# Token sums of the softmax over tokens for batches 0 and 1: added on GpSimd instead of by eight matmuls

## The chip, the cores and the metric

One core of one Trainium2 chip. The metric is the device time of the kernel in microseconds (us). Small differences are read twice: as ratios of timed runs with a 95% interval, and as moments inside the traces. Engine names in the profile: PE is TensorE, PEld its weight loads, DVE VectorE, ACT ScalarE, POOL GpSimd, SP SyncE (SPq its queue of transfer issues).

## The reference

`x` is 8 batches x 8 heads x 512 tokens x 64, `state` 8 x 8 x 32 x 64. What matters is the second attention, from state to tokens (two lines of the reference are joined here):

```python
scores2 = scale * np.matmul(state, x.transpose(0, 1, 3, 2))
a2 = np.exp(scores2 - scores2.max(-1, keepdims=True))
a2 /= a2.sum(-1, keepdims=True) + 1e-09      # sum over the 512 tokens
sread = np.matmul(a2, x)
```

The result (with the first attention's) goes through a gated layer `(sigmoid(x @ w_gate) * (x @ w_val)) @ w_out`, which is nearly all of the matmul work.

## The kernel before

Tokens lie as 128 partitions x 4 tokens, so the sum over 512 tokens is a sum over 4 in the partition and over 128 partitions. TensorE does the latter with a matrix of ones. `E1s` are the exponentials in fp32, `Ebs` the same in bf16.

```python
def at_Eb(b):                                  # GpSimd casts E1 to bf16
    Ebs[b] = ap_.tile((128, 4, 2, 4, Ns), BF, name="Eb")
    for c in range(4):
        nc.gpsimd.tensor_copy(Ebs[b][:, c], E1s[b][:, c])
...
def sr_mm(b, place):
    ...
    if b in Es:                                # batches 2 to 7: summed over c before
        terms = [(e, Es[b][:, k, e]) for e in range(2) for k in range(2)]
    else:                                      # batches 0 and 1
        terms = [(e, Eb[:, c, e]) for e in range(2) for c in range(4)]
    for i, (e, rhs) in enumerate(terms):
        nc.tensor.matmul(sm, ones[:, e], rhs, start=(i == 0), stop=(i == len(terms) - 1))
    for j in range(4):                         # then the unnormalised read, 16 matmuls
        ...
```

Each engine runs its instructions in program order. The order around the place, with cuts marked `...` (the comments are mine, here and above):

```python
    gv_glu(0, 4)
    at_Eb(0)
    load_x(2, nc.gpsimd)
    load_wo(0)
    load_wo(1)
    load_wo(2)
    load_x(3, nc.gpsimd)
    gv_glu(0, 5)
    ...
    sw_visit(1, 512, 512, 0)
    ...
    sr_mm(1, AT)                # TensorE's sum for batch 1
    ...
    gv_mm(1, 1, GV)             # GLU pair of feature block 1
    ...
    sr_mm(0, OU)                # and for batch 0, some 9 us later
    ...
    pad(2, 6)                   # GpSimd: two copies
    cast_x(2, pool, 0, 4)       # GpSimd: x of batch 2 to bf16
    cast_x(2, pool, 4, 4)
    cast_x(3, pool, 0, 4)
    cast_x(3, pool, 4, 4)
    at_xT_dma(2)                # SyncE: four transposing transfers, then the scores of batch 2
    at_xT_dma(3)
```

The softmax here doesn't subtract the row's maximum and nothing guards it: scores larger than these inputs give would overflow.

Of the kernel before, what the change touches and what calls it, by code (L numbers as in the profile page):

```python
# [8 lines left out]
FP = mybir.dt.float32  # L9
BF = mybir.dt.bfloat16  # L10
AF = mybir.ActivationFunctionType
ALU = mybir.AluOpType
# [4 lines left out]
def kernel(  # L17
# [14 lines left out]
    nc = tc.nc  # L32
    B, H, S, D = x.shape
    Ns = state.shape[2]
# [11 lines left out]
    ap_ = ctx.enter_context(tc.tile_pool(name="ap", bufs=2))  # L46
# [19 lines left out]
    Es, E1s, Ebs, abs_, aTs, SWs, glus = {}, {}, {}, {}, {}, {}, {}  # L66
    vec, act, pool = nc.vector.tensor_copy, nc.scalar.copy, nc.gpsimd.tensor_copy


    def load_x(b, eng, parts=1, hold=None):  # L70
        xf = stg.tile((128, H, 4, D), FP, name="xf")
        if hold is not None:

            hold.memset(xf[:, 0, 0, 0:1], 0.0)
        v = x[b].rearrange("h (p c) d -> p h c d", c=4)
        n = H // parts
        for i in range(parts):
            eng.dma_start(xf[:, n * i:n * i + n], v[:, n * i:n * i + n])
        xfs[b] = xf
# [16 lines left out]
    def load_wo(q):  # L96
        nc.gpsimd.dma_start(wo[:, 4 * q:4 * q + 4],
                            moe_w_out.rearrange("(k p) n -> p k n", p=128)[:, 4 * q:4 * q + 4])
# [57 lines left out]
    def n_tok(b, e):  # L156

        if e == 0:
            held["E4", b] = ap_.tile((128, 2, 4, Ns), FP, name="E4")
        nc.vector.tensor_reduce(held["E4", b][:, e].rearrange("p j n -> p (j n)"),  # L160
                                E1s[b][:, :, e].rearrange("p c j n -> p (j n) c"), AX.X, ALU.add)

    def n_split(b, k):

        if k == 0:
            Es[b] = ap_.tile((128, 2, 2, 4, Ns), BF, name="Es")
            nc.vector.tensor_copy(Es[b][:, 0], held["E4", b])
        else:
            nc.vector.tensor_tensor(Es[b][:, 1], held["E4", b], Es[b][:, 0], ALU.subtract)
# [105 lines left out]
    def sw_cp(b, lo, w, e, cp):  # L275
        cp(*sw_left.pop((b, lo, w, e)))  # L276


    def n_of(b):
        return 512 if b < B else B * Ns  # L280
# [21 lines left out]
    def gv_glu(b, f):  # L302
        if b not in glus:
            glus[b] = fp.tile((128, NF, n_of(b)), BF, name="glu", bufs=2, padded_shape=(128, NF, 512))
        nc.vector.scalar_tensor_tensor(glus[b][:, f], held["th", b, f], 1.0, held["gv", b, f][1], ALU.add, ALU.mult)  # L305
# [192 lines left out]
    load_wo(1)  # L498
    load_wo(2)
    load_x(3, nc.gpsimd)  # L500
    gv_glu(0, 5)
    sw_cp(1, 512, 1, 1, vec)
    sw_visit(1, 512, 512, 0)
# [72 lines left out]
    for b in range(1, B + 1):  # L576
        nb = b + 1 if b + 1 < B else None
        for f in range(NF):
# [14 lines left out]
            if nb is not None:  # L593
# [15 lines left out]
                if f in (6, 7):  # L609
                    n_tok(nb, f - 6)  # L610
                    if f == 7:
                        n_split(nb, 0)
                elif f == 8:
                    n_split(nb, 1)
                elif f == 9:
                    sr_mm(nb, AT)
                    sr_inv(nb)
                    if b == 1:
                        sr_fin(nb)
                elif f == 10 and b > 1:  # L620
                    sr_fin(nb)
# [48 lines left out]
```

## Time and profile before

| | before |
|---|---|
| time, median of 3 runs | 229.8 us (228.96 to 230.15) |
| TensorE busy | 95% of the span of 227.5 us |
| GpSimd busy | 20% |
| ones-matmuls of batches 0 and 1 | 2 x 8, holding TensorE's stream for 0.46 and 0.45 us |
| last transpose of batch 2 landed | 46.88 us, in one profile |

TensorE's busy share is close to full, so read the moments, not the shares: when does each block of TensorE's stream start, and what did it wait for. The lines are in the prediction.

### The profile page before, as it was taken

Reading aid. Unit: us, or ns where it says so; the run is one execution under the profiler, and the core shown is the slowest. Engines: PE = TensorE matmul, PEld = TensorE weight load, DVE = VectorE, ACT = ScalarE, POOL = GpSimd, SP = SyncE. Lnnn points to the kernel's source line nnn. Section 1 sums busy time; section 2 is a strip of 40 time slices with the busy share of each in tenths; the row PEclk is TensorE's granted clock in tenths of the full one; section 3 lists DMA queues with packets and bytes.
Section 4 is the critical chain, followed back from the end, with each engine's and each line's share of the span. In section 5 each row is a group of like instructions: output and inputs, shape, how many; then the busy total and the mean of one; then the engine's idle time right before and its main releaser. Section 6 shows DMA issues by size and latency. Waiting matters only on the chain.

```text
span 227.5 us, 4735 instructions
## 1 busy us (share of the span) xinstructions
PE 215.7 (95%) x1831; PEld 111.6 (49%) x1856; DVE 141.4 (62%) x234; ACT 131.0 (58%) x246; POOL 44.4 (20%) x78
## 2 busy tenths in 40 slices
PE   7568999999999999999999999999999999999994
PEld 7453345444454545444544454454445444466743
DVE  2599889967448855886488638874687433422301
ACT  3677877647476566746675666656755444423311
POOL 1499930060033001500060006000200000000001
PEclk9999999999999999999999999999999999999999
DMA  6999999943699252725282431243122111111113
GB/s 213 354 176 191 233 264 242 152 80 69 145 287 248 41 132 101 231 46 124 87 252 43 83 116 46 81 83 116 46 72 69 48 46 49 67 73 46 49 35 104
DMA packets 37990, 28.09 MB, mean 123 GB/s; under 512 B 20976, under 2 KB 33136, under 8 KB 37968
## 3 DMA queue, kind: packets, MB, share of 16 engines
q1 hardware_dynamic: 32464, 21.31, 35.3%
q0 software_dynamic: 5360, 6.42, 14.8%
q8 instruction: 14, 0.23, 0.4%
q14 instruction: 8, 0.07, 0.2%
q10 hardware_dynamic: 144, 0.07, 0.1%
HBM read 18.35 MB, written 8.91 MB: 120 GB/s over the span
## 4 chain that ended last, share of the span: by engine, by line
PE 76%; DMA 11%; POOL 5%; SPq 3%; issue 2%; ACT 1%; DVE 0%; POOLq 0%; ACTq 0%
PE outp L321 35%; PE gvp L290 28%; DMA xf<-in_x_dram 8%; PE gvp L293 5%; PE swp L238 4%; DMA xT<-xb 3%; SPq L128 2%; PE srp L215 1%; POOL Eb L145 1%; PE Sp L134 1%; PE outp L341 1%; POOL wg L83 1%; POOL ab L175 1%; POOL xb L103 1%; POOL wv L94 1%
## 5 line engine op out<-in xcount | busy, mean ns | idle before, releaser
L305 DVE SCALAR_TENSOR_TENSOR glu<-th,gvp 128x512 bf16<-128x512 f32 (+1 forms) x108 | 70.2, 657 | 63.9 <-ACT th L300 48.2
L300 ACT ACTIVATE th<-gvp 128x512 f32<-128x512 f32 (+1 forms) x108 | 61.6, 575 | 62.5 <-PE gvp L290 51.2
L290 PE MATMUL gvp<-aT,SW 128*128 128x512 bf16 x384 | 96.3, 379 | 0.2
L321 PE MATMUL outp<-wo,glu 128*128 128x512 bf16 x371 | 95.1, 379 | 1.3 <-issue 0.2
L290 PEld LDWEIGHTS <-SW 128*128 128x128 bf16 x384 | 36.2, 98 | 45.1 <-issue 4.2
L321 PEld LDWEIGHTS <-glu 128*128 128x128 bf16 x396 | 37.4, 98 | 40.7 <-issue 0.4
L276 ACT CAST SW<-swp 128x512 bf16<-128x512 f32 (+1 forms) x78 | 42.2, 582 | 4.2 <-PE swp L238 2.9
L145 POOL CAST Eb<-E 128x256 bf16<-128x256 f32 x32 | 12.4, 429 | 96.2 <-ACT E L139 96.2
L325 ACT ACTIVATE res<-outp 128x512 f32<-128x512 f32 x33 | 19.7, 598 | 17.1 <-PE outp L321 17.1
L103 POOL CAST xb<-xf 128x1024 bf16<-128x1024 f32 (+1 forms) x13 | 14.6, 1147 | 20.8 <-DMA xf<-in_x_dram 20.8
L276 DVE CAST SW<-swp 128x512 bf16<-128x512 f32 x20 | 13.4, 683 | 0.7 <-PE swp L238 0.7
L175 DVE TENSOR_TENSOR ab<-E,ri 128x512 bf16<-128x512 f32 x14 | 13.7, 980 | 0.1
L332 POOL DMA_DIRECT2D out_dram<-res x2 | 1.0, 526 | 60.1 <-ACT res L325 60.1
L160 DVE TENSOR_REDUCE E<-E 128x128 f32<-128x512 f32 x12 | 12.3, 1033 | 0.0
L152 DVE TENSOR_REDUCE rs<-E 128x16 f32<-128x512 f32 x16 | 10.8, 678 | 2.0 <-ACT E L139 2.0
L238 PE MATMUL swp<-wg,sTc 64*32 64x256 bf16 (+1 forms) x256 | 11.6, 328 | 0.3
L238 PEld LDWEIGHTS <-sTc 64*32 64x32 bf16 x512 | 6.4, 90 | 10.7 <-issue 7.9
L139 ACT ACTIVATE E<-Sp 128x512 f32<-128x512 f32 x16 | 9.6, 608 | 2.5 <-PE Sp L134 2.5
L238 PE MATMUL swp<-wv,sTc 64*32 64x256 bf16 (+1 forms) x256 | 10.3, 324 | 0.2 <-POOL wv L94 0.2
L220 DVE RECIPROCAL r<-srp 128x128 f32<-128x128 f32 x8 | 7.6, 951 | 1.5 <-PE srp L215 1.5
L134 PEld LDWEIGHTS <-xT 128*128 128x128 bf16 x128 | 5.7, 98 | 4.3 <-ACT xT L123 0.8
L134 PE MATMUL Sp<-sTz,xT 128*128 128x64 bf16 x128 | 6.4, 193 | 1.3 <-ACT xT L123 0.7
(54 smaller groups left out, 109.0 us busy)
## 6 DMA issues: line engine op xcount, KB each, us to landing
out_dram<-res SPq DMA_DIRECT2D x31, 256.0 KB, 2.5
xf<-in_x_dram SPq DMA_DIRECT2D x5, 1024.0 KB, 6.9
xf<-in_x_dram POOLq DMA_DIRECT2D x2, 1024.0 KB, 14.3
wo<-in_moe_w_out_dram POOLq DMA_DIRECT2D x3, 512.0 KB, 12.7
xf<-in_x_dram SPq DMA_DIRECT2D x2, 512.0 KB, 5.3
wg<-in_moe_w_gate_dram POOLq DMA_DIRECT2D x2, 512.0 KB, 7.1
wv<-in_moe_w_val_dram POOLq DMA_DIRECT2D x2, 512.0 KB, 7.7
sf<-in_state_dram SPq DMA_DIRECT2D x1, 512.0 KB, 3.7
```

The source lines that it names most:

```text
L103: cp(xbs[b].rearrange("p c h d -> p h c d")[:, lo:lo + n], xfs[b][:, lo:lo + n])
L134: nc.tensor.matmul(ps[:, c, :, jj], xTs[b][:, 2 * i + jj, c], sTz[:, b, 2 * i + jj], start=True, stop=True)
L145: nc.gpsimd.tensor_copy(Ebs[b][:, c], E1s[b][:, c])
L160: nc.vector.tensor_reduce(held["E4", b][:, e].rearrange("p j n -> p (j n)"), E1s[b][:, :, e].rearrange("p c j n -> p (j n) c"), AX.X, ALU.add)
L175: eng.tensor_tensor(abs_[b].rearrange("p c e (j n) -> p (c e) j n", n=Ns)[:, :, 2 * i:2 * i + 2], halfE(b, i), ri.unsqueeze(3).to_broadcas ...
L238: nc.tensor.matmul(pss[e][j * Ns:(j + 1) * Ns, o:o + n], sTc[rows, b, j], (wg, wv)[w][rows, j, lo:lo + n], start=True, stop=True)
L276: cp(*sw_left.pop((b, lo, w, e)))
L290: nc.tensor.matmul(ps, SWs[b][:, g, w, fs], aTs[b][:, :, g], start=(g == 0), stop=(g == 1))
L300: nc.scalar.activation(th, held["gv", b, f][0], AF.Tanh, scale=0.5)
L305: nc.vector.scalar_tensor_tensor(glus[b][:, f], held["th", b, f], 1.0, held["gv", b, f][1], ALU.add, ALU.mult)
L321: nc.tensor.matmul(ops[b, c], glus[b][:, f, c * 128:(c + 1) * 128], wo[:, f], start=(f == 0), stop=(f == NF - 1))
L325: nc.scalar.activation(res, ops[b, c], AF.Copy, scale=0.5)
```

## The change

The intent is to give TensorE less to do: two terms (a bf16 value and the bf16 remainder of the fp32 sum) in place of four tokens, four ones-matmuls a batch instead of eight, with the sum over the four tokens made by GpSimd, which is idle 80% of the time. The other batches do this on VectorE.

```diff
+    def p_tok(b):
+
+        E4, E5 = (ap_.tile((128, 2, 4, Ns), FP, name=f"P{i}", bufs=1) for i in range(2))
+        add = nc.gpsimd.tensor_tensor
+        add(E4, E1s[b][:, 0], E1s[b][:, 1], ALU.add)
+        add(E5, E1s[b][:, 2], E1s[b][:, 3], ALU.add)
+        add(E4, E4, E5, ALU.add)
+        Es[b] = ap_.tile((128, 2, 2, 4, Ns), BF, name="Es")
+        pool(Es[b][:, 0], E4)
+        add(Es[b][:, 1], E4, Es[b][:, 0], ALU.subtract)
@@ (in the order of the program)
     load_wo(2)
     load_x(3, nc.gpsimd)
+    p_tok(1)
+    p_tok(0)
     gv_glu(0, 5)
```

## The prediction

> **What bounds the kernel now.** I read the page first (engine shares, slices), then the chain of work that ended last in order of time, then the timelines of GpSimd and TensorE between 18 and 60 us, then the waits on TensorE, and last the transfers in flight around 45 us. The page:
>
> ```profile
> PE 215.7 (95%) x1831; PEld 111.6 (49%) x1856; DVE 141.4 (62%) x234; ACT 131.0 (58%) x246; POOL 44.4 (20%) x78
> PE   7568999999999999999999999999999999999994
> L212 PE MATMUL srp<-Es,ones x24: 219/219/219, 56.6 to 173.3; 128*128 128x128 bf16 x24
> L212 PE MATMUL srp<-Eb,ones x16: 219/219/229, 28.6 to 38.2; 128*128 128x128 bf16 x16
> ```
>
> The first two lines say that TensorE is the bound from about 20 us to the end, at full granted clock. So a change is worth what it takes off TensorE's stream or puts into it as a wait; GpSimd at 20% is only a supplier. The other two (the instructions of the line that makes the token sums, with least, median and largest duration) show what the change touches: 16 matmuls for batches 0 and 1 take the four tokens of Eb one by one, where the later batches take two terms of Es.
>
> TensorE's timeline around the two places, and the token sum of batch 2 for comparison:
>
> ```profile
> 28.21 0.42 PE L238 MATMUL swp<-wg,sTc 64*32 64x512 bf16 x8
> 28.57 0.62 PE L212 MATMUL srp<-Eb,ones 128*128 128x128 bf16 x8
> 29.03 0.63 PE L215 MATMUL srp<-Eb,xb 128*128 128x64 bf16 x16
> ...
> 37.81 0.61 PE L212 MATMUL srp<-Eb,ones 128*128 128x128 bf16 x8
> 38.26 0.63 PE L215 MATMUL srp<-Eb,xb 128*128 128x64 bf16 x16
> ...
> 46.62 0.86 PE L134 MATMUL Sp<-sTz,xT 128*128 128x64 bf16 x16
> ...
> 56.62 0.39 PE L212 MATMUL srp<-Es,ones 128*128 128x128 bf16 x4
> 56.84 0.63 PE L215 MATMUL srp<-Eb,xb 128*128 128x64 bf16 x16
> ```
>
> Read the starts, not the durations, since matmuls overlap: eight ones-matmuls hold the stream for 29.03 - 28.57 = 0.46 us (0.45 in the second), four hold it for 0.22. Batch 1's sum is wanted at 28.57 us. The same stretch on GpSimd:
>
> ```profile
> 21.44 1.43 POOL L145 CAST Eb<-E 128x256 bf16<-128x256 f32 x4
> 22.81 0.90 POOL L78 DMA_DIRECT2D xf<-in_x_dram  x1
> 23.70 2.24 POOL L97 DMA_DIRECT2D wo<-in_moe_w_out_dram  x3
> 25.90 0.94 POOL L78 DMA_DIRECT2D xf<-in_x_dram  x1
> 26.79 1.76 POOL L391 COPY sTz<-sTc 64x768 bf16<-64x768 bf16 x2
> 32.08 2.02 POOL L103 CAST xb<-xf 128x1024 bf16<-128x1024 f32 x2 [3.53 <-DMA xf<-in_x_dram]
> 45.50 2.02 POOL L103 CAST xb<-xf 128x1024 bf16<-128x1024 f32 x2 [11.40 <-DMA xf<-in_x_dram]
> ```
>
> The new work goes in after the last load (25.90) and before the padding (26.79). Both facts that matter are here: it can't begin before 26.79, only 1.8 us ahead of TensorE's need, and GpSimd has 3.53 us of idle time before the cast of batch 2, which is less than two sums will need. What hangs on that cast is in the chain of work that ended last:
>
> ```profile
> 32.08 2.03 POOL xb L103 x2
> 34.11 0.02 issue
> 34.12 1.29 SPq L128
> ...
> 39.74 7.14 DMA xT<-xb
> 46.88 0.05 issue
> 46.93 0.33 PE Sp L134 x5
> ```
>
> Cast, four transposes issued by SyncE, the last landing at 46.88, and then batch 2's scores. TensorE's wait there is only 0.2 us, so at 46.6 two paths arrive together: TensorE's own gapless stream from 20 us on, and this transfer chain. Either can delay what follows.
>
> **What the Trainium skill says.** Three places bear on it.
> "GPSIMD Engine Reference", section 3.1 Elementwise: a two-input elementwise operation takes about 2.6 cycles an element, 4497 ns for 2048 fp32 elements (2.2 ns each). The trace: GpSimd's products for `ab`, 512 elements, have a median of 1063 ns, 2.08 ns each. It agrees.
> "SBUF — State Buffer", section Who interferes with whom: a VectorE instruction with two SBUF inputs contends with a GpSimd instruction that reads SBUF; one with at most one SBUF input, outside the two-port modes, doesn't. The trace agrees: VectorE's `ab` product, median 710 ns, takes 1.76 us at 13.65 and 1.88 us at 17.82, just where GpSimd's own products lie (13.78, 17.07). Between 26.8 and 34 us VectorE runs only the GLU (one input in PSUM) and copies out of PSUM, so I expect neither side to slow down.
> "DMA: Bandwidth & Descriptors", section Queues, rings and completion order: each DMA engine takes turns between the queues that have work, packet by packet. This says why the transposes take 7.14 us here against a median of 2.5 from issue to landing: they share the engines with GpSimd's loads of wo and of x for batch 3, whose landing is what lets the cast at 45.50 start. The packets from 43.8 us on:
>
> ```profile
> q1 hardware_dynamic: 1206, 0.28, 84.9%
> q0 software_dynamic: 1, 0.00, 0.0%
> ```
>
> GpSimd's queue (q0) is drained by then, and 1206 packets of SyncE's (q1) are left; the transposes end together when the backlog ends. The trace agrees with taking turns.
>
> **The change part by part.**
> Removed: four ones-matmuls per batch, twice. Each batch saves 0.46 - 0.22 = 0.24 us of TensorE's stream, 0.47 in all. This lies fully on the path.
>
> Added on GpSimd per batch: three fp32 adds of 256 elements, one cast of 256 elements to bf16, one subtraction. The cast of this size has a median of 400 ns (Eb). A cast of 512 takes 0.61 and of 1024 1.04 us, so the fixed part is near 0.18; a two-input operation on 256 then takes (1.063 - 0.18)/2 + 0.18 = 0.62 us. Sum: 4 x 0.62 + 0.40 = 2.88 us. Neighbours overlap by about 0.05 us (four Eb casts cover 1.43, not 1.6), so 2.7 us in a row, 5.4 for both batches.
>
> Batch 1: 26.79 + 2.7 = 29.5 for the second term. The ones-matmuls would start at 28.57; the first can go once the cast is done, the second needs the subtraction. TensorE so waits about 0.9 us at a place where it had not waited. Net there: +0.9 - 0.24 = about +0.65 us.
> Batch 0: ready at 26.79 + 5.4 = 32.2, wanted at about 38.4. No wait, -0.24. TensorE's stream reaches the scores of batch 2 about 0.4 us later than before.
>
> Moved: padding to 32.2..34.0, cast of batch 2 to 34.0..36.0 (x itself landed before 32.08 and is not what it waits for now). The first transpose is issued 1.9 us later, at 36.0. This doesn't pass on in full. In quiet times four transposes issued 1.3 us apart from 36.0 would land by 36.0 + 3 x 1.3 + 2.5 = 42.4; what holds them to 46.9 is the backlog, and the bytes in it stay the same. Its end slips by whatever the transposes no longer get done beside the loads: they had moved some 840 of their 2048 data packets before 43.8, and if a third to a half of these are left over, 280 to 420 packets at about 450 a us (1206 in 2.7 us) make 0.6 to 0.9 us. Against that, the loads, less disturbed, end slightly earlier. I put the landing at 47.0 to 47.8, against TensorE's arrival at 46.6 + 0.4 = 47.0.
>
> Sum: the scores of batch 2 start between +0.3 and +0.9 us later, +0.6 in the middle. From there on TensorE is 95% or more busy in every stretch, with the same work in the same order; nothing catches the delay up. The batch 3 cast waits for its own load at 45.50 and is not moved by the new work. The transposes of `aT` for batch 2 stand behind eight `xT` transposes in SyncE's queue and end just ahead of their use near 59.9; if the queue slips more than TensorE does, a few tenths could show there too.
>
> **The rivals.**
> First, the saving is all that counts: GpSimd is idle 80% of the time and the added work hides. Then 229.3 us (-0.47). For it: TensorE is the bound and loses eight matmuls. Against it: 26.79 plus three serial adds, a cast and a subtraction can't be before 28.57.
> Second, the transfer chain passes the whole 1.9 us on: the transposes' landing moves from 46.88 to 48.8. Then about 231.7. For it: the chain of waits runs right through this cast. Against it: the 7.14 us, which is backlog, not latency.
> Third, the fp32 adds run at twice my estimate because of VectorE, as the products at 13.65 did: each sum 5.5 us, TensorE waits near 3.5 us, the cast slips by 7 us; about 233 to 234. Against it: no VectorE instruction with two SBUF inputs lies in this stretch.
>
> **Range and chances.** 229.8 + 0.6 = 230.4 us. The three runs of before differ by 1.2 us, so the median alone can move by half a microsecond; from the first rival to the second is 229.3 to 231.7. I take 229.5 to 231.7 for 8 in 10. Two per cent is 4.6 us: a gain of that size has no source (0.47 us is all there is to save), and a loss of that size needs more than the third rival. Faster 0.01, same 0.96, slower 0.03.
>
> **What would show it.** In the changed kernel: TensorE with a new wait of about 0.9 us at the ones-matmuls of batch 1, put down to GpSimd's subtraction; none at batch 0's; ones-matmuls on Es 40 and on Eb none; the two-input operations on 256 elements near 0.62 us, both sums over at 32.2; the cast of batch 2 at 34.0; the scores of batch 2 at 47.0 to 47.8; the span near 228.1 instead of 227.5. I am wrong if the wait at batch 1 is under 0.3 us (sums faster than I think), if the scores start after 48.3 (delay passed on), or if the delay at 47 us is gone again by the end.

## The result, and the profile after

| | before | changed |
|---|---|---|
| median of 6 runs | 229.66 us (228.96 to 230.15) | 230.46 us (230.26 to 231.4) |
| ratio | | 1.0043, 95% interval 1.0018 to 1.0067 |
| span of the profiled run | 227.5 us | 228.7 us |

Ratios here and below are the mean time of one kernel's fast runs over that of the other's of the same rounds, so not quite the ratio of the medians. Executions over 1.5% slower than the fastest of the same kernel are left out of the means. 1.0043 is about +1.0 us. By the mark of 2% it is the same time; the interval says that it is a little slower all the same.

TensorE's timeline of the changed kernel (start us, duration us, engine, line, operation, tiles, number of instructions; in brackets how long the engine was idle before and what ended that):

```profile
28.24 0.42 PE L249 MATMUL swp<-wg,sTc 64*32 64x512 bf16 x8
29.64 0.22 PE L223 MATMUL srp<-Es,ones 128*128 128x128 bf16 x1 [0.98 <-POOL Es L171]
30.39 0.33 PE L223 MATMUL srp<-Es,ones 128*128 128x128 bf16 x3 [0.53 <-POOL Es L172]
30.56 0.63 PE L226 MATMUL srp<-Eb,xb 128*128 128x64 bf16 x16
...
39.34 0.39 PE L223 MATMUL srp<-Es,ones 128*128 128x128 bf16 x4
39.56 0.63 PE L226 MATMUL srp<-Eb,xb 128*128 128x64 bf16 x16
```

From 19.9 to 28.2 us the two kernels agree within 0.03 us. Then TensorE waits twice, for the cast and for the subtraction of batch 1's sum. The block of ones-matmuls could have begun at 28.60 (0.36 us after the block ahead of it, as before) and the next begins at 30.56: 1.96 us, where before it was 0.46, so +1.50 with the saving already in it. (The idle time in the brackets adds up to 1.51 us. Against the 0.22 of four ones-matmuls without a wait the block took 1.74 us more, since matmuls that wait no longer overlap their neighbours.) Batch 0's has no wait and is 0.22 long instead of 0.45.

GpSimd in the same stretch of the changed kernel:

```profile
26.87 0.78 POOL L167 TENSOR_TENSOR P<-E 128x256 f32<-128x256 f32 x1
27.56 0.76 POOL L168 TENSOR_TENSOR P<-E 128x256 f32<-128x256 f32 x1
28.40 0.73 POOL L169 TENSOR_TENSOR P<-P,P 128x256 f32<-128x256 f32 x1
29.19 0.40 POOL L171 CAST Es<-P 128x256 bf16<-128x256 f32 x1
29.67 0.67 POOL L172 TENSOR_TENSOR Es<-P,Es 128x256 bf16<-128x256 f32 x1
...
35.56 2.02 POOL L103 CAST xb<-xf 128x1024 bf16<-128x1024 f32 x2
43.94 2.03 POOL L103 CAST xb<-xf 128x1024 bf16<-128x1024 f32 x2 [6.36 <-DMA xf<-in_x_dram]
```

A sum takes 26.87 to 30.34 us, 3.47 us. Look at the starts: a dependent instruction starts 0.06 to 0.08 us after the one before it has ended (28.40 against 27.56 + 0.76), while the two independent additions overlap by 0.09. The cast of batch 2 is 3.5 us late (35.56 for 32.08; its x had landed at 33.33), and the cast of batch 3 is 1.6 us *early* (43.94 for 45.50).

The shares of the span that each engine has in the chain of work that ended last, first the kernel before, then the changed one:

```profile
PE 76%; DMA 11%; POOL 5%; SPq 3%; issue 2%; ACT 1%; DVE 0%; POOLq 0%; ACTq 0%
```

```profile
PE 83%; POOL 8%; DMA 4%; issue 1%; ACT 1%; SPq 1%; DVE 0%; POOLq 0%; ACTq 0%
```

The transposes of batch 2 have left the chain (DMA 11 to 4%, SPq 3 to 1%) although the cast ahead of them is later: by the trace's landing times the last of them lands at 46.65 us instead of 46.88 (a difference that chance alone can make, see experiment 12), and TensorE comes to the scores at 47.88 without a wait. Before, the scores took 46.62 to 47.32, 0.70 us with their wait; now 47.88 to 48.35, 0.47.

So in the profiles: +1.50 (batch 1) - 0.23 (batch 0) - 0.23 (no wait at the scores) = +1.04 us. Measured from the weight visit at 28.2 to the end of TensorE's last block, 224.28 - 28.21 = 196.07 us before and 225.45 - 28.24 = 197.21 after: +1.14, so a tenth is unexplained, and two profiles of the same kernel differ by 0.48 in this measure (experiment 12). I call this stretch "the stream" below, since it leaves out what differs by chance before 28 us.

### The profile page after: what moved, and what is told of

It reads as the page before. It is cut to its first block, busy times and chain, and to the rows that moved or that the text cites. A ratio compares the mean times of both kernels' runs of the same rounds, so it can differ in the third digit from the quotient of the medians.

```text
span 228.7 us, 4731 instructions
## 1 busy us (share of the span) xinstructions
PE 216.2 (95%) x1823; PEld 111.3 (49%) x1848; DVE 140.8 (62%) x234; ACT 131.2 (57%) x246; POOL 50.9 (22%) x88
## 4 chain that ended last, share of the span: by engine, by line
PE 83%; POOL 8%; DMA 4%; issue 1%; ACT 1%; SPq 1%; DVE 0%; POOLq 0%; ACTq 0%
PE outp L332 36%; PE gvp L301 34%; PE gvp L304 5%; PE swp L249 4%; DMA xf<-in_x_dram 4%; PE srp L226 2%; POOL Eb L145 1%; PE outp L352 1%; PE Sp L134 1%; POOL wg L83 1%; POOL wo L97 1%; POOL ab L186 1%; PE srp L223 1%; POOL wv L83 1%; POOL xf L78 1%
## 5 line engine op out<-in xcount | busy, mean ns | idle before, releaser
L186 DVE TENSOR_TENSOR ab<-E,ri 128x512 bf16<-128x512 f32 x14 | 13.2, 943 | 0.1
```

The costliest lines, as they stand in the source:

```text
L186: eng.tensor_tensor(abs_[b].rearrange("p c e (j n) -> p (c e) j n", n=Ns)[:, :, 2 * i:2 * i + 2], halfE(b, i), ri.unsqueeze(3).to_broadcas ...
```

## The experiments

The theory after the result: TensorE's wait for batch 1's sum is the whole loss; GpSimd's delay of the cast costs nothing, because the transposes are held by the loads that are still under way (the backlog). The rival: the late cast passes on. All diffs are against the changed kernel unless said otherwise.

**1. The work without the wait.** The sums go to a tile that nobody reads.

```diff
-        Es[b] = ap_.tile((128, 2, 2, 4, Ns), BF, name="Es")
-        pool(Es[b][:, 0], E4)
-        add(Es[b][:, 1], E4, Es[b][:, 0], ALU.subtract)
+        Ed = ap_.tile((128, 2, 2, 4, Ns), BF, name="Ed", bufs=1)
+        pool(Ed[:, 0], E4)
+        add(Ed[:, 1], E4, Ed[:, 0], ALU.subtract)
```

> GpSimd makes both token sums as in the changed kernel, but writes them to a tile that nobody reads; the ones-matmuls take the four tokens of Eb as before. So GpSimd's delay is kept and TensorE's wait is taken away. Theory (the wait alone costs the time; the transposes of batch 2 are held by the backlog of loads whatever the time of their issue): no wait at the ones-matmuls, cast of batch 2 at about 35.5 us instead of 32.1, landing still at 46.5 to 47.0, time as before within 0.3 us (ratio 0.999 to 1.002). Rival (the late cast passes on through the transposes): ratio 1.004 or more, with the added time in front of the scores of batch 2.

229.22 us against 229.69 of before, ratio 0.9981 (0.9952 to 1.001). The chain from 26 us to the scores, in order of time (start us, us, what; with cuts), has TensorE all through:

```profile
28.86 0.55 PE srp L223 x8
...
39.11 6.17 PE gvp L301 x28
45.28 1.73 PE outp L332 x8
47.00 0.25 PE Sp L134 x8
```

The cast starts at 35.57, just as in the changed kernel, and the last transpose lands at 45.27, sooner than in any other run. The stream is 224.26 - 28.46 = 195.80 us, 0.27 *less* than before, about the wait at the scores (0.23) that is gone. The rival has fallen for a delay of 3.5 us: it needed a ratio of 1.004. GpSimd's added 7 us alone cost nothing that the interval shows.

**2. The same work twice**, to find where the backlog no longer hides the cast.

```diff
-    p_tok(1)
-    p_tok(0)
+    p_tok(1)
+    p_tok(0)
+    p_tok(1)
+    p_tok(0)
```

(with the unread tile of experiment 1)

> The same with the unread sums made twice, some 14 us of GpSimd instead of 7. Theory: the backlog hides a late cast only until it is drained; the cast of batch 2 ends near 44.6, four transposes issued 1.3 us apart then land near 44.7 + 3.9 + 2.5 = 51.1, so TensorE waits some 4.3 us at the scores of batch 2 and the time is 1.8 to 2.0 per cent longer than before. Rival (the late cast passes on in proportion): about twice what the kernel with the unread sums once shows. Third (that chain sets nothing): ratio near 1.000 again.

234.78 us, ratio 1.0223 (1.0193 to 1.0253): slower, though the interval holds the mark of 2%. TensorE's timeline of this kernel at the scores of batch 2:

```profile
47.40 0.20 PE L134 MATMUL Sp<-sTz,xT 128*128 128x64 bf16 x1 [0.31 <-DMA xT<-xb]
48.72 0.20 PE L134 MATMUL Sp<-sTz,xT 128*128 128x64 bf16 x1 [1.12 <-DMA xT<-xb]
50.02 0.24 PE L134 MATMUL Sp<-sTz,xT 128*128 128x64 bf16 x1 [1.09 <-DMA xT<-xb]
51.34 0.87 PE L134 MATMUL Sp<-sTz,xT 128*128 128x64 bf16 x13 [1.08 <-DMA xT<-xb]
```

Now it waits for each of the four transposes, 1.3 us apart, the last landing at 51.29 (51.1 was worked out beforehand): this is the pace of the transposes alone, since the loads had landed by 44.22. The idle times add up to 3.6 us, while the median rose by 5.1 and this profile's stream, 230.65 - 28.52 = 202.13 us, by 6.06. The trace has the rest. First, the whole block of scores cost 4.39 more: TensorE would have come to it at 46.93 (1.73 us after the start of the block ahead, as before) and left it at 52.02, 5.09 us, against 0.70 before. Second, the blocks behind it ran slower with the same work, here the kernel before and then this one:

```profile
47.32 1.03 PE L321 MATMUL outp<-wo,glu 128*128 128x512 bf16 x4
```

```profile
52.02 1.90 PE L332 MATMUL outp<-wo,glu 128*128 128x512 bf16 x4
```

The trace gives TensorE a granted clock of 0.50 from 49.2 to 56.0 us, and 1.00 from 12 to 49.2 and after 56.0. From 52.02 to 58.31 this cost 1.66 us (6.29 instead of 4.63), and 4.39 + 1.66 is the 6.06 to 0.01. (The profiled run is the longest of the six, at 235.67 us and a mean granted clock of 0.977 against 0.983 to 0.992 in the others, so these have probably lost less. What lowered the clock was not tested; it fell while TensorE waited.) The step is not in proportion, though: twice the work cost 5 us, once the work nothing. The slack of the cast lies between 3.5 and 10.7 us.

**3. The saving without the work.** Against the kernel before:

```diff
-            terms = [(e, Eb[:, c, e]) for e in range(2) for c in range(4)]
+            terms = [(e, Eb[:, c, e]) for e in range(2) for c in range(2)]
```

> Wrong on purpose: the kernel before, with only two of the four tokens of Eb in the ones-matmuls of batches 0 and 1, so four matmuls a batch and no work on GpSimd. This is the saving alone. Theory: 0.47 us is taken off TensorE's stream, but TensorE then waits at the scores of batch 2 until the transposes land near 46.9, so the gain is 0 to 0.2 us (ratio 0.999 to 1.000). Rival (TensorE's stream is the only bound): the whole 0.47 us, ratio 0.998.

228.99 us, ratio 0.9981 (0.9948 to 1.0015), relative error 0.033 as was to be expected. The stream is 223.69 - 28.08 = 195.61, 0.46 less than before: the size of the whole saving in this profile, where I had expected the transposes to eat most of it. They landed at 46.30. My expectation took the 46.88 of one profile for a fixed moment.

**4. Batch 1 alone** (the line `p_tok(0)` taken out).

> The change for batch 1 alone, the one whose sum comes too late. Theory: the wait of 1.5 us in two pieces stays as in the changed kernel, batch 0 keeps its eight ones-matmuls, so the time is about 0.24 us over that of the changed kernel: ratio to before 1.0050 to 1.0060. Rival (GpSimd's delay of the cast counts): the cast is only 1.8 us late here instead of 3.5, so the time would be below that of the changed kernel.

230.45 us, ratio 1.0033 (1.0006 to 1.0061). The two waits are 0.95 and 0.53 us, nearly those of the changed kernel, and the time is that of the changed kernel, not 0.24 more; the interval is too wide to tell. The stream is 197.31, 0.10 more than the changed kernel's. The cast starts 2.5 us earlier here (33.10), which bought nothing: the last transpose landed at 47.69.

**5. Batch 0 alone** (the line `p_tok(1)` taken out).

> The change for batch 0 alone, the one whose sum is needed 10 us after it can be ready. GpSimd: one sum of 3.5 us (as measured), ready at 30.4, the cast of batch 2 hardly later than before (near 32.2). Theory (the wait at batch 1 is the whole loss): no wait at any ones-matmul, 0.23 us off TensorE's stream between the first ones-matmul and the scores of batch 2; the time is that of before or up to 0.25 us less, ratio 0.998 to 1.000. Rival (any work put there on GpSimd costs): ratio 1.002 or more.

229.45 us against 229.76, ratio 0.9983 (0.9947 to 1.0019), no wait at a ones-matmul. The stream is 224.00 - 28.43 = 195.57, 0.50 less than before: 0.23 saved at batch 0, 0.23 at the scores. Experiments 4 and 5 together put the loss on batch 1: the six runs of 4 take 230.39 to 230.95 us, those of 5 229.02 to 230.08.

**6. The sum wanted later.** One call moved on TensorE, so that other work fills the wait.

```diff
-    sr_mm(1, AT)
     ...
     gv_glu(1, 1)
+    sr_mm(1, AT)
     gv_mm(1, 6, GV)
```

> The changed kernel with one call moved: TensorE makes batch 1's sums after the two next visits and the GLU pair of feature block 1, when Es is ready (30.4 us) or nearly so. Theory: the waits of 0.98 and 0.53 us shrink to under 0.3 together, both savings stay, TensorE's stream comes to the scores of batch 2 some 0.3 to 0.45 us earlier than in the kernel before, and the transposes, issued at 37.6, land by then (45.3 to 46.7 in the runs so far); ratio to before 0.9975 to 0.9995. Rival (the late cast costs as well): the scores of batch 2 then wait for the transposes and the ratio is 1.000 or more.

229.26 us, ratio 0.9979 (0.9943 to 1.0014), so 1.2 us under the median of the changed kernel. No wait for the sum is left. The profiled run was the longest of the six (230.22) and has two other waits: 0.6 us for a weight load (wv, landed at 30.77) that TensorE now reaches sooner, and 0.3 for the transposes (landed at 47.66). I had not thought of the first.

**7. The cast ahead of batch 0's sum**, on top of 6.

```diff
-    p_tok(0)
     ...
     cast_x(2, pool, 4, 4)
+    p_tok(0)
     cast_x(3, pool, 0, 4)
```

> As the last, and batch 0's sum on GpSimd put behind the cast of batch 2, so that the cast starts at 32.2 as before and the sum still comes before it is wanted at 38. If the late cast costs, this is faster than the last by what it costs (up to 0.5 us). Theory (the landing is held by the backlog and was, if anything, sooner with the later issue): no faster than the last, the landing at 46.5 to 47.0, a wait of up to 0.5 us at the scores of batch 2, ratio to before 0.9985 to 1.000.

230.50 us, ratio 1.0019 (0.9981 to 1.0058): unclear. The edit has a fault: batch 0's `sr_mm` is emitted ahead of this `p_tok(0)`, finds no `Es` and takes the eight tokens of Eb, so that saving is lost. What it does show: the cast starts at 33.07, 2.6 us earlier than in experiment 6, and the transposes land at 47.53 against 47.66. So an earlier cast bought 0.1 us here, which is within chance. Its profiled run (230.64) also has a wait of 1.22 us for a weight load at 25.3, ahead of everything that was edited. Why its median is over that of 6 stays open.

**8. A wider first addition.**

```diff
-        add(E4, E1s[b][:, 0], E1s[b][:, 1], ALU.add)
-        add(E5, E1s[b][:, 2], E1s[b][:, 3], ALU.add)
-        add(E4, E4, E5, ALU.add)
+        add(P2, E1s[b][:, 0:2], E1s[b][:, 2:4], ALU.add)
+        add(E4, P2[:, 0], P2[:, 1], ALU.add)
```

(the lines that make the tiles left out)

> The changed kernel with the first two additions of 256 elements made one of 512, so one instruction less a sum. If a good part of an addition's 0.73 to 0.78 us is fixed, 512 elements take about 1.3 us and the sum 3.3 instead of 3.5 us; the wait at batch 1 shrinks from 1.5 to 1.3 us and the time by 0.2 us, ratio to before 1.003 to 1.004. If the time is all by the element (3 ns each), 512 take 1.5 us and nothing is gained.

The wide addition takes 1.32 us (1.27 for batch 0), the sum 27.00 to 30.35, 3.35 instead of 3.47 us; the waits are 0.84 and 0.53. The stream is 197.05, 0.16 less than the changed kernel's. The median is 230.38 us, ratio 1.0020 (0.9983 to 1.0057): the timing can't resolve it, the trace agrees with a fixed part in each instruction.

**9. The disputed cost by itself.** The kernel before, with seven instructions more where GpSimd was idle (the edit in short: tiles left out, the last line abridged).

```diff
     cast_x(2, pool, 4, 4)
+    for n in (128, 256, 512):
+        mt(mf[:, 0:n], Ef[:, 0:n], Ef[:, 512:512 + n], ALU.add)      # fp32 result
+        mt(mb[:, 0:n], Ef[:, 0:n], Ef[:, 512:512 + n], ALU.add)      # bf16 result
+    mt(mb (16 x 32), Ef[:, 0:512] (16 x 32), Rf.unsqueeze(2).to_broadcast((128, 16, Ns)), ALU.mult)
```

> The kernel before with seven more two-input instructions on GpSimd behind the cast of batch 2, where it was idle, of 128, 256 and 512 elements, each once with an fp32 and once with a bf16 result, and one product of 512 whose second input is repeated over 32 elements like that of ab. It measures the size that the prediction took from ab. Theory (the prediction scaled the wrong kind: the repeated input is cheaper to read than two full inputs): the product takes 1.06 us, the full additions 1.25 us or more at 512 and 0.67 to 0.78 at 256. Rival (VectorE or the loads slowed the additions of the changed kernel): the additions here take 1.06 at 512 and 0.62 at 256, like ab.

Groups of GpSimd's instructions in this stretch, shapes kept apart (count | busy us, mean ns of one | idle before):

```profile
L588 POOL TENSOR_TENSOR mf<-E 128x512 f32<-128x512 f32 x1 | 1.3, 1263 | 0.0
L590 POOL TENSOR_TENSOR mb<-E,ri 128x512 bf16<-128x512 f32 x1 | 1.0, 1046 | 0.1
L588 POOL TENSOR_TENSOR mf<-E 128x256 f32<-128x256 f32 x1 | 0.7, 712 | 0.0
L588 POOL TENSOR_TENSOR mf<-E 128x128 f32<-128x128 f32 x1 | 0.4, 444 | 0.0
```

The sizes bear the theory out. From 128 to 512 elements an addition of two full inputs grows by (1263 - 444) / 384 = 2.13 ns an element, which leaves 0.17 us fixed; the bf16 results take the same (445, 718, 1262). The product with a repeated second input takes 1046 for 512, as `ab` does. The prediction had the fixed part right and took the element's price from the cheaper kind. What makes that kind cheaper is only argued: the product differs from the additions in the repeated input and also in multiplying, and no product of two full inputs was run. (One run, 229.15 us, state unknown; only its trace is used.)

**10. Batch 1's sum ahead of the loads**, so that it is ready in time.

```diff
     at_Eb(0)
+    p_tok(1)
     load_x(2, nc.gpsimd)
     ...
     load_x(3, nc.gpsimd)
-    p_tok(1)
     p_tok(0)
```

> The changed kernel with batch 1's sum on GpSimd put ahead of the loads of x for batch 2, of wo and of x for batch 3 (batch 0's sum stays behind them). The sum is then ready at about 26.4 us, before TensorE wants it at 28.6; those loads are issued 3.5 us later. Theory (only the wait costs, and GpSimd's load queue is still busy with the weights until 29 to 30.8, so a later issue of the next loads moves nothing much): no wait at the ones-matmuls, cast of batch 2 near 35.6, transposes landed by 47, time 229.0 to 229.5, ratio to before 0.997 to 0.999. Rival (late loads cost): wo or x of batch 3 late, TensorE waits at the scores or at the first output rows, ratio 1.001 or more.

230.72 us, ratio 1.0022 (0.9977 to 1.0067): unclear, and not the gain that I expected. The profiled run was a slow one (232.78 us), so I explain nothing from it; it has no wait for the sum, but 2.0 us of waits for the transposes, which landed at 47.49 to 48.87, behind x of batch 3 at 47.31, and then a granted clock of 0.50 from 49.2 to 52.7 us. The six runs go from 229.12 to 232.78, the widest of all. Whether the loads, issued 3.4 us later, cost the fast runs anything stays open, since none of them was profiled.

**11. The sum one block later**, the dose of the wait.

```diff
-    sr_mm(1, AT)
     ...
     gv_mm(1, 1, GV)
+    sr_mm(1, AT)
```

> The changed kernel with TensorE's sum of batch 1 one block later, behind the GLU pair of feature block 1 (0.93 us of other work). The dose of the wait: it shrinks by 0.93 us, from 1.5 to about 0.6 in all, and the time by the same: about 229.5 us, ratio to before 0.999 to 1.001. If the time does not follow the wait, the wait is not what costs.

229.47 us, ratio 0.9985 (0.9951 to 1.002), 1.0 us under the changed kernel, as expected. In the profiled run no wait for the sum is left, where I expected 0.6 us: TensorE itself came 0.8 us late, having waited for a weight load:

```profile
24.94 0.41 PE L249 MATMUL swp<-wv,sTc 64*32 64x512 bf16 x8 [0.82 <-DMA wv<-in_moe_w_val_dram]
...
30.31 0.39 PE L223 MATMUL srp<-Es,ones 128*128 128x128 bf16 x4
```

**12. The kernel before as a kernel of its own.**

> The kernel before, unchanged, as a kernel of its own: how far do medians of six runs differ by chance? Expected ratio 1.000 with an interval of some 0.3 per cent either side, a spread of more than 1 us between its runs; if its profiled run is one of the long ones, TensorE should show a wait for the last weight load (wv) near 30.7 us that the profile of the kernel before does not have.

229.76 us, ratio 1.0007 (0.9971 to 1.0043): this is how far chance goes. The long wait on wv that I expected is not in its profile; the transposes landed at 47.40 instead of 46.88, TensorE waited 0.27 us there, and the stream is 196.55, 0.48 longer than in the first profile of the same kernel. So the differences of the stream in experiments 1, 3, 4, 5 and 8 (0.10 to 0.50 us) could each be chance; what stands is the start and length of single blocks, and the runs.

Five kernels without TensorE's wait for the sum have medians of 228.99 (3), 229.22 (1), 229.26 (6), 229.45 (5) and 229.47 us (11); those with it 230.38 (8), 230.45 (4) and 230.46 (changed). No run of the five is above 230.22 us, and none of the three is below 230.19. Two more kernels without that wait do not fit: 7 (230.50, its edit faulty) and 10 (230.72). Their runs spread over 1.8 and 3.7 us, and their profiled runs have other waits in the wait's place (1.22 us for a weight load; 2.0 us for the transposes, in a slow run). Whether their other runs have these too is not shown. The kernel before lies at 229.50 to 229.76. So 5, 6 and 11, which keep the work and lose the wait, are about a microsecond below the changed kernel, but none is shown to beat the kernel before: all their intervals hold 1.

## Why the prediction was right or wrong

The time was right (230.4 predicted, 230.46 measured, inside 229.5 to 231.7), and so was its main mechanism: TensorE, which had not waited, waits for GpSimd's sum of batch 1. Step by step:

- *Saving of 0.24 us a batch*: right. Batch 0's block went from 0.45 to 0.22 us, and with the saving alone (experiment 3) the stream lost 0.46.
- *A sum takes 2.7 us*: too small, 3.47 measured. This is the mis-sized term. The durations add up to 3.34 instead of 2.88. Of these 0.46 us, 0.37 are there because an addition of two full inputs costs 2.13 ns an element and not the 1.72 taken from `ab`, a product whose second input is repeated (experiment 9: 0.71 us for 256 elements, 0.62 predicted, four times); why the first two additions took 0.78 and 0.76 us is open. The other 0.33 us is the spacing: I took 0.05 of overlap at each of four boundaries from independent casts, but three of the four are dependent and have a gap of 0.06 to 0.08.
- *TensorE waits about 0.9 us, +0.65 net*: 0.98 + 0.53 measured, +1.50 net. This follows from the last point.
- *VectorE does not slow the additions*: right. The Trainium skill ("SBUF — State Buffer", Who interferes with whom) named which VectorE instructions would; in this stretch there were none, and the additions took 0.67 to 0.78 us, against 0.71 for the same size in experiment 9. (The prediction's own sign of this contention was read loosely: VectorE's product at 17.82 lay beside the last 0.31 us of GpSimd's product and then beside casts of Eb, not beside a product all through.)
- *The first transpose is issued 1.9 us later, and the landing slips to 47.0 to 47.8*: wrong, there was no slip. The issue came at 37.61, 3.5 us later, and the landing at 46.65. I had weighed the leftover packets as +0.6 to +0.9 us and the relief of the loads as slight; in fact x of batch 3 landed at 43.82 instead of 45.38, which, as I read it, left the engines to the transposes that much sooner. In the five profiles of fast runs with a cast near 35.5 us (1, 6, 8, 11 and the changed one) the last transpose landed at 45.27 to 47.66, in the six with a cast near 33 or before (before, 3, 4, 5, 7, 12) at 46.30 to 47.69. These ranges overlap: the later cast brought no later landing, but it is not shown to bring an earlier one.
- *What holds them to 46.9 is the backlog*: right in that an earlier issue did not help, but the word hides something. In all 13 profiles (the slow one of 10 and the one of 9 among them) whose transposes were issued before x of batch 3 had landed, the first transpose landed 0.16 to 1.42 us after that load (before: 45.56 after 45.38). And little was left to move by then: in the kernel before 281 GB/s from 40 to 42 us and 66 from 42 to 44. So the transposes end behind the last packets of one load; why is not shown. "The trace agrees with taking turns" holds only in part: issued at 34.12, the transposes moved no packet until 38.05 while the loads moved some 770, and with no load about (experiment 2) the first packet followed 1.26 us after the issue.
- *The cast of batch 3 is not moved by the new work*: wrong in this profile, where its x landed sooner: 43.94 instead of 45.50. With the same work on GpSimd it started at 45.18 in experiment 6, and in the kernel before at 46.02 in experiment 12.
- *Nothing catches the delay up*: nearly right. The stream's +1.50 - 0.23 lost another 0.23 at the scores, where the old wait was, and the rest was there at the end.

So that 230.4 came so close to 230.46 is in part luck: the net wait was 0.85 us under-sized, and the slip of the landing, which doesn't exist, made up for a part. Among the signs that the prediction named, the scores began at 47.88 and not by 47.8, both sums were over at 33.85 and not at 32.2, and "ones-matmuls on Es 40" was added up wrongly: 24 + 2 x 4 is 32, and the trace has 32.

The first rival (only the saving counts) fell with the wait at 29.64. The second (the cast passes on in full) fell with experiment 1; even a cast 10.7 us late cost 5.1 (experiment 2). The third (additions at twice the time) fell with their durations.

One observation is only argued: the kernels with the wait have tight runs (8: 230.19 to 230.48; five of six of the changed one within 230.26 to 230.58), the kernel before and several without it spread by over 1 us. A wait whose end GpSimd sets would swallow TensorE's chance delays ahead of it, such as the 0.82 and 1.22 us for weight loads in 11 and 7. That would also make the average loss smaller than the wait. No run was made to test it.

## What to carry to other kernels

An idle engine is not a free one: ask when its result is *wanted*, and lay the chain of its instructions, with their gaps, from the moment that it can start. Here 3.5 us of serial work began 1.7 us ahead of its reader on the bound engine, and moving the reader by one block took the loss away. And look behind a long wait too: in experiment 2 the granted clock stood at 0.50 for another 4 us after TensorE had gone on, for 1.66 us of loss that no wait shows. A transfer that ends behind other transfers can have slack that its place in the chain of waits does not show; delay it in an experiment before you pay for an earlier issue.

## What the Trainium skill lacked or had wrong

- "GPSIMD Engine Reference", section 3.1 Elementwise: its 2048-element figure (4497 ns) agrees with the runs' 2.13 ns an element and 0.17 us fixed (an estimate of 4.53 us from these), but it gives no small sizes of a two-input operation (444, 712 and 1263 ns for 128, 256 and 512 elements, so 0.17 us fixed) and doesn't say that a product with a repeated second input is cheaper (1046 ns for 512).
- "GPSIMD Engine Reference", section 2.1 Instruction dispatch, asks for a wait between dependent instructions across cores, but doesn't say what a dependent chain costs: here a gap of 0.06 to 0.08 us after the end of the one before, where independent ones overlapped by 0.03 to 0.09.
- "DMA: Bandwidth & Descriptors", section Queues, rings and completion order, tells how queues take turns, but no page what follows for a later issue: in one pair of profiles transposes issued 3.5 us later landed 0.2 us sooner, and the load that they shared the engines with landed 1.6 us sooner; over 11 profiles of fast runs the last landing was at 45.27 to 47.66 us with the later issue and at 46.30 to 47.69 with the earlier one.
